# Loading the first chunk's values from ScalarE's queue, and filling a gap of TensorE with four constant products

## The chip, the core and the metric

The kernel runs on one core of a Trainium2 chip. The metric is the device time of one execution in microseconds (us). Five engines work side by side, each through its own instructions in order: TensorE (PE; its weight loads are shown apart as PEld), VectorE (DVE), ScalarE (ACT), GpSimd (POOL) and SyncE (SP), whose instructions here are nearly all transfers (DMAs). Engines wait for one another and for transfers on semaphores.

## What is computed

An attention whose heads are mixed before and after the softmax, and behind it two layers of weights each with an activation of its own:

```python
# batch 2, 12 heads, sequence 448, head size 64
scores = scale * np.matmul(q, k.transpose(0, 1, 3, 2))
scores = np.einsum('bhij,hg->bgij', scores, w_pre)      # premix
attn = softmax(scores)
attn = np.einsum('bhij,hg->bgij', attn, w_post)         # postmix
x = np.matmul(attn, v)                                   # then 896 tokens x 768
h = x @ w1_in;  x = (h * np.clip(h + 3, 0, 6) / 6) @ w1_out
h = x @ w2_in;  out = (P(h) / (Q(h) + 1e-06)) @ w2_out
```

All inputs are float32. A product of two float32 operands is done as three products of their high and low parts.

## The kernel before

The attention is cut into eight chunks: four of up to 120 query rows for each batch. Chunk C is cut into groups of ten rows (twelve groups in chunks 0 to 2, nine in chunk 3); a group holds 10 rows x 12 heads = 120 partitions, so that the mixing of heads is one product with a 120 x 120 matrix. Groups are counted through all chunks as m: chunk 0 has m = 0 to 11, chunk 1 begins with m = 12.

For each chunk, `scores` makes the products of queries and keys for two heads at a time (tiles `sc`); ACT and DVE copy them to a staging tile `stg`, and two DMAs on SP's queue (line 249, `spread`) rearrange them into the tile `full`, in which the twelve heads of a group lie on 120 partitions. Twelve such DMAs of 210 KB make the `full` of a chunk. Only for chunk 0 they go another way: one DMA for each group (line 252), out of a tile `stage`. The six pairs of heads of chunk 1 are called stg_0 to stg_5 below; the first three are made ahead of the loop over groups (`FIRST = 3`, line 503).

A step of the loop takes one group: `gsplit` (POOL, lines 290 and 292) splits group m+3 of `full` into `sh` and `sl`; `premix` (PE, lines 302 to 304, tile `M`) mixes the heads of group m; DVE takes the maximum (line 306), ACT the exponential `e` (line 308) and the scaled weights `wr` (line 321); `postmix` (PE, line 337, tile `A`) mixes group m-2. Work for the next chunk (its `scores`) and for the chunk before (`av_unit`, line 359: the product with the values, tile `X`) is dealt to steps by small tables. The order on every engine is that of the code (`manual_schedule`) from here on.

The first split of each chunk reads `full`, whose last spreads must have landed: POOL waits there for all of the chunk's spreads.

The values `vraw` are loaded for pairs of heads, 224 KB each, into four buffers (`load_v`, line 130). The first four loads, for chunk 0, are issued on SP's queue in step 3 of chunk 1 (line 596); the fifth and later ones follow as `av_unit` gives a buffer back. The first `av_unit` of chunk 0 runs in step 7 of chunk 1.

The DMAs of all queues are dealt to eight lanes (semaphores `DMAHW0` to `DMAHW7`) in turn, at the time the program is built. A DMA is issued only when the DMA that had its lane before it has landed; the wait stands on the issuing engine, in its order.

Ahead of everything, eleven bf16 products on a constant tile `warm` run on PE (line 150). Between the last `scores` made ahead and the first `premix`, PE waits for the first group's spread and split.

Of the kernel before, what the change touches and what calls it, by code (L numbers as in the profile page):

```python
# [7 lines left out]
F32 = mybir.dt.float32  # L8
# [11 lines left out]
B, H, S, D = 2, 12, 448, 64  # L20
# [9 lines left out]
def plan():  # L30

    chunks, parts = [], []
    for b in range(B):
        for c in range(NCH):
            n = min(CH, S - c * CH)
            G = (n + GR - 1) // GR
            parts.append([(0, G)])
            chunks.append((b, c * CH, n, G))  # L40
    return chunks, parts
# [7 lines left out]
def fused_kernel(  # L49
# [15 lines left out]
    nc = tc.nc  # L65
    NT, DM = out.shape
    DFF = w1_out.shape[0]
    WARM = 11
    KD = DM // 128
    KF = DFF // 128  # L70
    GLAG = 1
# [1 line left out]
    chunks, parts = plan()  # L73
# [30 lines left out]
    ps = tc.alloc_tile_pool(name="ps", bufs=2, space=PSUM)  # L104
# [22 lines left out]
        nc.sync.dma_start(out=t, in_=k[b, :, 2 * m : 2 * m + 2])  # L127
        kraw[(b, m)] = t

    def load_v(C, hp):  # L130
        if C < len(chunks) - 1:
            t = att.tile([JP, 2, JC * D], F32, tag="vraw", bufs=4, name=f"vraw{C}_{hp}")
            nc.sync.dma_start(out=t, in_=v[chunks[C][0], hp])
            vraw[(C, hp)] = t

    def load_vs():
# [9 lines left out]
    warm = front.tile([128, 512], BF16, name="warm")  # L146
    nc.vector.memset(warm, 0.0)
    pw = ps.tile([128, 512], F32, tag="A", name="warm_ps")
    for i in range(WARM):
        nc.tensor.matmul(pw, lhsT=warm[:, :128], rhs=warm, start=(i == 0), stop=(i == WARM - 1))  # L150
    for m in range(3):
# [6 lines left out]
    for i, w in enumerate((w_pre, w_post)):  # L158
        nc.sync.dma_start(
            out=wrep[:, i, :], in_=w[None, :, :].to_broadcast([GR, H, H])  # L160
# [52 lines left out]
    def room(n):  # L213
        while posts and sum(banks_of) + n > BUFS["sc"]:
            banks_of.pop(0)
            for p in posts.pop(0):
                p()

    def post(n, *parts):
        banks_of.append(n)  # L220
        posts.append(parts)

    def flush():
        room(BUFS["sc"] + 1)
        while xposts or preps:
            for p in (xposts or preps).pop(0):
                p()
# [9 lines left out]
    def q_prep(C, p0=0, p1=NP):  # L237
        ns = chunks[C][3] * GR
        hi, lo, src = (x[:, p0:p1, :ns] for x in (qr, ql, qraw[C]))
        preps.append([  # L240
            lambda: nc.scalar.activation(out=hi, in_=src, func=AF.Copy),
            lambda: nc.vector.tensor_tensor(out=lo, in0=src, in1=hi.bitcast(F32), op=ALU.subtract),
        ])
# [10 lines left out]
    def scores(C, hp, tags=("sc", "sc"), st=None, first=nc.scalar.copy,  # L254
               second=nc.vector.tensor_copy):
        n = chunks[C][3] * GR
        kh, kl = kst[:, 0, hp, :], kst[:, 1, hp, :]
        if hp == 0:
            full[C] = att.tile([GP, MG, S], F32, tag="full", bufs=2, name=f"full{C}")
        room(2)  # L260
        sc = [ps.tile([128, 512], F32, tag=t, bufs=BUFS[t], name=f"sc{C}_{2 * hp + i}") for i, t in enumerate(tags)]
        far = st is None
        if far:
            st = front.tile([CH, 2, S], F32, tag="raw", bufs=5, name=f"stg{C}_{hp}")
        for j, (w, x) in enumerate(((qr, kh), (ql, kh), (qr, kl))):
            for i in range(2):
                o = slice(i * D, i * D + D)
                nc.tensor.matmul(sc[i][:n, :S], lhsT=w[o, hp, :n], rhs=x[o], start=(j == 0), stop=(j == 2))  # L268

        def take(i, copy):  # L270
            copy(out=st[:n, i], in_=sc[i][:n, :S])
            if far:
                spread(C, 2 * hp + i, st[:, i])

        post(2, lambda: take(0, first), lambda: take(1, second))

    ssp = {}

# [225 lines left out]
    q_prep(1, 0, FIRST)  # L504
    flush()
    for hp in range(FIRST):
        scores(1, hp)
        flush()
    q_prep(1, FIRST, NP)
    flush()  # L510
    gsplit(0, nc.vector)()
# [14 lines left out]
    def gemm1(f, p, hp):  # L526
        hps[(f, p)] = hp
        return gemm_in(p, hp, spl[("in1", f, 0)])
# [40 lines left out]
    for C, (b, r0, n, G) in enumerate(chunks):  # L569
        nxt = C + 1 if C + 1 < len(chunks) else None  # L570
        sched = {}

        def add(units, steps):
            for i, u in enumerate(units):
                sched.setdefault(steps[i * len(steps) // len(units)], []).append(u)

        sst = SST[G] if C else ONES
        if nxt is not None:
            kw = {} if C else {"first": nc.vector.tensor_copy}
            add([lambda h=h: scores(nxt, h, **kw) for h in range(0 if C else FIRST, NP)], sst)  # L580
        if C + 2 < len(chunks):
            add([lambda: q_prep(C + 2, 0, NP // 2), lambda: q_prep(C + 2, NP // 2, NP)], QST[G] if C else [6, 8])
        if C == NCH - 2:
            add([lambda m=m: load_k(1, m) for m in range(3)], [6, 7, 9])
            add([lambda h=h: k_prep(1, h) for h in range(4)], [9, 10, 10, 11])
        if C == NCH - 1:
            add([lambda h=h: k_prep(1, h) for h in range(4, NP)], [0, 1])
        if C > 0:
            add([lambda h=h: av_unit(C - 1, h) for h in range(1, H, 2)], [("av", a) for a in (AVST[G] if nxt is not None else AVLAST)])

        for s in range(G):
            if s == (5 if C == 1 else 0) and C and C + 2 < len(chunks):
                load_q(C + 2)
            if C == 1 and s == 3:
                for i in range(4):
                    load_v(0, i)
            if C == 2 and s == 3:
                load_ab()
            if C == 3 and s == 0:
                build_ab()  # L600
            while aposts:
                aposts.pop(0)()
            if full_step:
                norm(m - 1)
                weigh(m - 1)
            for p in posts[:1] + xposts:
                p[0]()
            gsplit(m + 3)()
            if C:
                for p in posts[:1]:  # L610
                    p[1]()
            premix(m)
            if m == 0:
                low()
            if not C:
                for p in posts[:1]:
                    p[1]()
            if m >= 1 and not full_step:
                norm(m - 1)
                weigh(m - 1)  # L620
            for p in posts[1:]:
                p[0]()
            for p in posts[1:]:
                p[1]()
            full_step = bool(s in sst if nxt is not None else s >= 7) or ("av", s) in sched
            for p in xposts + lows:
                p[1]()
            for p in preps:
                p[0]()
            lows[:] = preps  # L630
            preps.clear()
            xposts.clear()
            posts.clear()
            banks_of.clear()
            if C > PRE or (C == PRE and s == G - 1):
                next(wpieces)
            if m >= LAG:
                postmix(m - LAG)
            for u in sched.get(("av", s), []):
                u()  # L640
            for u in sched.get(s, []):
                u()
            if C == PRE and s == LATE - 1:
                flush()
                front.release()
                pools["late"] = tc.alloc_tile_pool(name="late", bufs=1, side="right", reuse_waits="tile")
                load_units(1)
                wpieces = (p for u in units[:4] for p in split_pieces(u))
            if C == PRE and s >= LATE:
                x_move(s - LATE, 0, XEAR)  # L650
            if C > PRE and s < KD - 3:
                x_move(s + 3, 0, XEAR)
            if C > PRE and s == 3:
                x_move(slice(0, KD), XEAR, XRAW)
            if C > PRE and s == 1:
                load_vs()
            if C > PRE and s == 4:
                load_units(2)
            if nxt is None and s >= 7:
                if s == 7:  # L660
                    h100 = gemm1(0, 0, ps.tile([128, 512], F32, tag="sc", bufs=BUFS["sc"], name="h1_0_0"))
                for _ in range(3):
                    next(h100)
            m += 1

    C = len(chunks) - 1
# [77 lines left out]
    for c in range(KD):  # L744
        hp = [bank(f"y1_{c}_{p}") for p in range(2)]
# [76 lines left out]
    for f in range(KF):  # L822
        advance(ui)
        w = spl.pop(("in2", f, 0))
# [8 lines left out]
        hp = hps[0]  # L833
# [5 lines left out]
        if f == 0:  # L839
            hp = hps[1]  # L840
            run(gemms[1])
        else:
            hp = bank2(tags[1], f"h2_{f}_1")
# [54 lines left out]
    for t in range(NB0):  # L898
        o = gp.tile([TB, DM], F32, tag="o", bufs=3, name=f"o0_{t}")
# [15 lines left out]
    for t in range(NB1):  # L915
        row = P0 + t * TB
        o = gp.tile([TB, DM], F32, tag="o", bufs=3, name=f"o1_{t}")
# [61 lines left out]
```

## Time and profile before

| | |
|---|---|
| median of three runs | 713.1 us (712.63 to 716.39) |
| the profiled execution | 713.87 us, its span 712.1 us |
| PE busy in the span | 696.0 us (98%) |
| DVE, ACT, POOL busy | 558.1, 412.3, 256.0 us |
| DMA queue of SP | 121.66 MB, 54.2% of 16 engines' span |
| mean granted clock of TensorE | 0.994 of full speed |

The busy time of PE says little by itself, since products are pipelined and their ends are modelled. What matters here is where PE stands still, what it waits for there, and the two places in the attention where its granted clock is at half.

### The profile page before, as it was taken

The page shows a single profiled execution, that of the slowest core. Times are in us where ns is not written, and L with a number is a line of the kernel's source. Part 1 is how long each engine was busy: PE and PEld are TensorE (multiplying, and loading weights), DVE is VectorE, ACT ScalarE, POOL GpSimd, SP SyncE. Part 2 cuts the span into 40 slices and gives each one's busy share as a digit, 9 for nine tenths or more (in the row PEclk, how much of TensorE's full clock was granted, in tenths as well). Part 3 has the DMA queues.
Part 4 walks back from the last instruction along what each step waited for, and adds up shares of the span by engine and source line. Part 5 has one row for each costly group of instructions (what it writes and reads, how often), then busy time and mean ns, then how long its engine had stood idle before and what let it go on. Part 6 is the DMA issues. An engine that isn't in the chain of part 4 may idle for free.

```text
span 712.1 us, 12398 instructions
## 1 busy us (share of the span) xinstructions
PE 696.0 (98%) x4457; PEld 620.7 (87%) x4457; DVE 558.1 (78%) x933; ACT 412.3 (58%) x851; POOL 256.0 (36%) x255
## 2 busy tenths in 40 slices
PE   8998999999999999999999999999999999999997
PEld 4778888888889888989888888879999999989997
DVE  6754675665657589899997777888988899899991
ACT  6776787777888443435332211246676767579851
POOL 2884864977776334332444443410000000000000
PEclk9999999999999999999999999999999999999999
DMA  6636486555394454555354554364657666855522
GB/s 201 228 98 184 129 209 181 165 145 177 108 250 139 129 160 133 155 156 156 119 185 142 183 183 140 115 208 169 210 192 240 214 230 212 310 187 200 185 83 88
DMA packets 76032, 122.81 MB, mean 172 GB/s; under 512 B 6804, under 2 KB 56260, under 8 KB 75972
## 3 DMA queue, kind: packets, MB, share of 16 engines
q1 hardware_dynamic: 75684, 121.66, 54.2%
q8 instruction: 35, 0.57, 0.4%
q10 hardware_dynamic: 288, 0.37, 0.1%
q14 instruction: 25, 0.20, 0.1%
HBM read 83.39 MB, written 19.27 MB: 144 GB/s over the span
## 4 chain that ended last, share of the span: by engine, by line
PE 47%; DVE 31%; DMA 10%; issue 5%; ACT 5%; POOL 0%; SPq 0%; ACTq 0%; DVEq 0%; POOLq 0%
PE A L337 9%; DVE wf L431 7%; DVE wf L427 7%; PE X L359 5%; PE acc L385 4%; PE sc L268 4%; PE acc L384 4%; PE acc L383 4%; DMA pre<-wf 4%; DVE gl L550 4%; DVE wf L425 4%; DMA wraw<-in_moe_w_in_dram 4%; PE M L302 3%; PE h L384 3%; PE h L385 3%
## 5 line engine op out<-in xcount | busy, mean ns | idle before, releaser
L385 PE MATMUL h<-xh,wl 128*128 128x512 f32 (+1 forms) x384 | 140.9, 367 | 0.8 <-DVE wl L451 0.7
L384 PE MATMUL h<-xl,wh 128*128 128x512 f32 (+1 forms) x384 | 140.8, 367 | 0.5 <-DVE xl L759 0.5
L383 PE MATMUL h<-xh,wh 128*128 128x512 f32 (+1 forms) x384 | 141.1, 367 | 0.0
L423 ACT ACTIVATE wf<-wraw 128x768 f32<-128x768 f32 (+1 forms) x56 | 48.6, 877 | 96.6 <-DMA pre<-wf 56.5
L292 POOL TENSOR_TENSOR sl<-full,sh 120x448 fp32r<-120x448 f32 x87 | 99.9, 1149 | 7.3
L306 DVE TENSOR_REDUCE st<-M 120x1 f32<-120x448 f32 x90 | 56.0, 622 | 53.9 <-PE M L304 53.6
L337 PEld LDWEIGHTS A<-wr,e 120*112 120x112 f32 x720 | 87.4, 178 | 7.4 <-ACT wr L321 3.1
L337 PE MATMUL A<-wr,e 120*112 120x120 f32 x720 | 89.5, 268 | 1.7 <-ACT wr L321 1.7
L447 POOL TENSOR_SCALAR wh<-wf 128x768 fp32r<-128x768 f32 (+1 forms) x34 | 32.6, 960 | 140.7 <-DVE wf L431 135.1
L308 ACT ACTIVATE e<-M,st 120x448 f32<-120x448 f32 x90 | 57.1, 634 | 41.8 <-DVE st L306 34.8
L385 PEld LDWEIGHTS h<-xh,wl 128*128 128x128 f32 x384 | 72.2, 188 | 10.2 <-DVE wl L451 1.7
L384 PEld LDWEIGHTS h<-xl,wh 128*128 128x128 f32 x384 | 72.2, 188 | 8.7 <-DVE xl L759 0.9
L383 PEld LDWEIGHTS h<-xh,wh 128*128 128x128 f32 x384 | 72.2, 188 | 8.0
L385 PE MATMUL y<-gh,wl 128*128 128x384 f32 x192 | 70.9, 369 | 1.1 <-POOL wl L448 1.1
L290 POOL TENSOR_SCALAR sh<-full 120x448 fp32r<-120x448 f32 x87 | 53.3, 612 | 49.9 <-PE M L303 19.8
L383 PE MATMUL y<-gh,wh 128*128 128x384 f32 x192 | 70.5, 367 | 0.0
L384 PE MATMUL y<-gl,wh 128*128 128x384 f32 x192 | 69.9, 364 | 0.0
L448 POOL TENSOR_TENSOR wl<-wf,wh 128x768 fp32r<-128x768 f32 (+1 forms) x34 | 67.7, 1990 | 2.8
L427 DVE SCALAR_TENSOR_TENSOR wf<-wraw,icst,wf 128x768 int32<-128x768 int32 (+1 forms) x56 | 61.8, 1103 | 1.0
L425 DVE TENSOR_SCALAR wf<-wf 128x768 int32<-128x768 int32 x66 | 42.4, 642 | 23.0 <-ACT wf L423 22.4
L431 DVE SCALAR_TENSOR_TENSOR wf<-wraw,icst,wf 128x768 int32<-128x768 int32 (+1 forms) x56 | 57.7, 1031 | 0.6
L549 ACT ACTIVATE gh<-g 128x384 fp32r<-128x384 f32 (+1 forms) x32 | 18.6, 581 | 60.3 <-DVE g L547 59.9
(109 smaller groups left out, 1524.2 us busy)
## 6 DMA issues: line engine op xcount, KB each, us to landing
wraw<-in_moe_w_out_dram SPq DMA_DIRECT2D x28, 768.0 KB
wraw<-in_moe_w_in_dram SPq DMA_DIRECT2D x22, 768.0 KB
full<-stg SPq DMA_DIRECT2D x60, 210.0 KB
vraw<-in_v_dram SPq DMA_DIRECT2D x42, 224.0 KB
wpre<-in_moe_w_in_dram SPq DMA_DIRECT2D x10, 768.0 KB
w2h<-wh SPq DMA_DIRECT2D x16, 384.0 KB
w2l<-wl SPq DMA_DIRECT2D x16, 384.0 KB
wsh<-w2h SPq DMA_DIRECT2D x16, 384.0 KB
```

What stands on the lines that cost most here:

```text
L290: eng.tensor_scalar(out=sh[:r], in0=s[:r], scalar1=1.0, scalar2=0.0, op0=ALU.mult, op1=ALU.add)
L292: return lambda: eng.tensor_tensor(out=sl[:r], in0=s[:r], in1=sh[:r].bitcast(F32), op=ALU.subtract)
L306: nc.vector.tensor_reduce(out=st[:r, 0:1], in_=mt[:r, :S], op=ALU.max, axis=AX.X, negate=True)
L308: nc.scalar.activation(out=e[:r], in_=mt[:r, :S], func=AF.Exp, bias=st[:r, 0:1], accum_out=st[:r, 1:2])
L337: nc.tensor.matmul(av[:, jc], lhsT=e[:r, jc * JP : (jc + 1) * JP], rhs=wr[:r, :, :rr], start=True, stop=True)
L383: nc.tensor.matmul(o, lhsT=wh, rhs=mh, start=first, stop=False)
L384: nc.tensor.matmul(o, lhsT=wh, rhs=ml, start=False, stop=False)
L385: nc.tensor.matmul(o, lhsT=wl, rhs=mh, start=False, stop=last)
L425: nc.vector.tensor_scalar(out=wi, in0=wi, scalar1=3, scalar2=None, op0=ALU.logical_shift_left)
L427: nc.vector.scalar_tensor_tensor(out=wi, in0=hw, scalar=icst[:, 0:1], in1=wi, op0=ALU.bitwise_and, op1=ALU.bitwise_or)
L431: nc.vector.scalar_tensor_tensor(out=wi, in0=lw, scalar=icst[:, 1:2], in1=wi, op0=ALU.logical_shift_right, op1=ALU.bitwise_or)
L448: nc.gpsimd.tensor_tensor(out=lv, in0=w, in1=hv.bitcast(F32), op=ALU.subtract)
```

## The change

Two edits. The first four loads of values are issued on ScalarE's queue at the end of the last step of chunk 0 instead of on SP's queue in step 3 of chunk 1. And four bf16 products on the constant tile `warm`, with 512 columns each, are put behind the last product of the `scores` made ahead; `issue_after` ties them to that place of PE's order.

```diff
-    WARM = 11
+    WARM, GAP = 11, 4
-    def load_v(C, hp):
+    def load_v(C, hp, eng=nc.sync):
...
-            nc.sync.dma_start(out=t, in_=v[chunks[C][0], hp])
+            eng.dma_start(out=t, in_=v[chunks[C][0], hp])
...
     for hp in range(FIRST):
-        scores(1, hp)
+        mm = scores(1, hp)
         flush()
+    pw = ps.tile([128, 512], F32, tag="A", name="gap_ps")
+    with tc.issue_after(mm.ins):
+        for i in range(GAP):
+            nc.tensor.matmul(pw, lhsT=warm[:, :128], rhs=warm, start=(i == 0), stop=(i == GAP - 1))
...
-            if C == 1 and s == 3:
-                for i in range(4):
-                    load_v(0, i)
...
+            if C == 0 and s == G - 1:
+                for i in range(4):
+                    load_v(0, i, nc.scalar)
```

On SP's queue, the spreads of stg_2 to stg_5 of chunk 1 (rows 24 to 31 of that queue) with the semaphores for which each waits. Before:

```order
L249 DMA full_270<-stg_2_299 10x12x448 [waits DMAHW4_49,Activation_49]
L249 DMA full_270<-stg_2_299 10x12x448 [waits DMAHW5_49,DVE_49]
L249 DMA full_270<-stg_3_356 10x12x448 [waits DMAHW6_49,DVE_49]
L249 DMA full_270<-stg_3_356 10x12x448 [waits DMAHW7_49,DVE_49]
L249 DMA full_270<-stg_4_413 10x12x448 [waits DMAHW0_49,DVE_49]
L249 DMA full_270<-stg_4_413 10x12x448 [waits DMAHW1_49,DVE_49]
L249 DMA full_270<-stg_5_470 10x12x448 [waits DMAHW2_49,DVE_49]
L249 DMA full_270<-stg_5_470 10x12x448 [waits DMAHW3_49,DVE_49]
```

The same eight rows in the changed kernel:

```order
L249 DMA full_270<-stg_2_299 10x12x448 [waits DMAHW0_49,Activation_49]
L249 DMA full_270<-stg_2_299 10x12x448 [waits DMAHW1_49,DVE_49]
L249 DMA full_270<-stg_3_361 10x12x448 [waits DMAHW2_49,DVE_49]
L249 DMA full_270<-stg_3_361 10x12x448 [waits DMAHW3_49,DVE_49]
L249 DMA full_270<-stg_4_418 10x12x448 [waits DMAHW4_49,DVE_49]
L249 DMA full_270<-stg_4_418 10x12x448 [waits DMAHW5_49,DVE_49]
L249 DMA full_270<-stg_5_475 10x12x448 [waits DMAHW6_49,DVE_49]
L249 DMA full_270<-stg_5_475 10x12x448 [waits DMAHW7_49,DVE_49]
```

The order on SP is the same, but every one of these spreads has moved by four lanes: four DMAs have been dealt lanes 4 to 7 between stg_1 (lanes 0 to 3) and stg_2.

On ACT, in the changed kernel, the rows around the four loads; `e_611` and `wr_615` belong to m = 11 and m = 10, the last of chunk 0, and `e_641` to m = 12, the first of chunk 1:

```order
L309 ACTIVATE e_611,st_609<-M_605,st_609 120x448 [waits DVE_49]
L322 ACTIVATE wr_615<-wq,st_586 120x120 [waits DVE_49,Activation_49]
L133 DMA vraw_0_622<-in_v_dram 112x512 [waits DMAHW4_49]
L133 DMA vraw_1_624<-in_v_dram 112x512 [waits DMAHW5_49]
L133 DMA vraw_2_626<-in_v_dram 112x512 [waits DMAHW6_49]
L133 DMA vraw_3_628<-in_v_dram 112x512 [waits DMAHW7_49]
L309 ACTIVATE e_641,st_639<-M_635,st_639 120x448 [waits DVE_49]
```

These are the four DMAs that hold lanes 4 to 7. In the built program the count for which stg_4's first spread waits on lane 4 is 64, and the load vraw_0 waits there for 48 and brings it to 64; so the load has the lane ahead of the spread, and likewise vraw_1 to vraw_3 ahead of the three spreads behind it.

On PE, in the changed kernel, the end of the scores made ahead and the first premix:

```order
L268 MATMUL sc_5_298<-xh,qr 120x448
L513 LDWEIGHTS warm
L513 MATMUL gap_ps<-warm 128x512
L513 LDWEIGHTS warm
L513 MATMUL gap_ps<-warm 128x512
L513 LDWEIGHTS warm
L513 MATMUL gap_ps<-warm 128x512
L513 LDWEIGHTS warm
L513 MATMUL gap_ps<-warm 128x512
L303 MATMUL M_334<-sh_317,wp_h 120x448 [waits DVE_49,Pool_49]
```

Before, the row of `M` stood directly behind that of `sc_5`; the four products wait for nothing.

## Rows read from the trace of the kernel before

**Rows 1.** The page: span and instructions.

```profile
span 712.1 us, 12398 instructions
```

**Rows 2.** PE's timeline (start, us, engine, line, out<-in, count [idle before <-releaser]), 1 to 28 us.

```profile
1.24 4.87 PE L150 MATMUL warm_ps<-warm 128*128 128x512 bf16 x11 [1.24 <-DVE icst L172]
...
15.35 0.44 PE L302 MATMUL M<-sh,wp_h 120*120 120x448 f32 x1 [1.00 <-DVE sh L290]
...
17.39 0.68 PE L268 MATMUL sc<-xh,qr 64*120 64x448 f32 x2
...
21.19 0.44 PE L302 MATMUL M<-sh,wp_h 120*120 120x448 f32 x1
...
22.79 0.46 PE L268 MATMUL sc<-xh,qr 64*120 64x448 f32 x2
...
25.04 0.44 PE L302 MATMUL M<-sh,wp_h 120*120 120x448 f32 x1
```

**Rows 3.** Stretches: busy us of PE, PEld, DVE, ACT, POOL; granted clock, DMA share, GB/s.

```profile
14.00:15.00 1.00, 0.35 (x3) 0.00 (x0) 0.19 (x1) 0.53 (x1) 0.00 (x0) 1.00 0.65 251
...
18.00:19.00 1.00, 1.00 (x7) 0.44 (x4) 0.76 (x3) 0.66 (x3) 0.92 (x2) 0.50 0.66 244
```

**Rows 4.** POOL's timeline, the first split of chunk 1.

```profile
37.59 0.56 POOL L290 TENSOR_SCALAR sh<-full 120x448 fp32r<-120x448 f32 x1 [3.73 <-PE A L337]
```

**Rows 5.** Stretches around the first split of chunk 1, columns as in rows 3.

```profile
36.00:37.00 1.00, 1.00 (x10) 0.91 (x9) 0.24 (x2) 0.85 (x4) 0.00 (x0) 1.00 0.05 18
37.00:44.00 7.00, 5.72 (x40) 4.02 (x38) 3.65 (x13) 4.13 (x12) 6.08 (x8) 1.00 0.01 4
```

**Rows 6.** PE's timeline at the first group of chunk 1.

```profile
38.21 0.46 PE L302 MATMUL M<-sh,wp_h 120*120 120x448 f32 x1 [0.65 <-POOL sh L290]
...
39.43 0.47 PE L304 MATMUL M<-sl,wp_h 120*120 120x448 f32 x1 [0.56 <-POOL sl L292]
```

**Rows 7.** SP's timeline: issues of transfers (start, us, line, count), from several stretches.

```profile
0.79 0.39 SPq L157 DMA_DIRECT2D kraw<-in_k_dram  x1
...
11.95 0.86 SPq L252 DMA_DIRECT2D full<-stage  x1
...
29.18 0.76 SPq L249 DMA_DIRECT2D full<-stg  x1
...
31.74 0.85 SPq L249 DMA_DIRECT2D full<-stg  x1
...
48.47 1.89 SPq L133 DMA_DIRECT2D vraw<-in_v_dram  x4
```

**Rows 8.** ACT's timeline at the end of chunk 0.

```profile
38.06 0.39 ACT L321 ACTIVATE wr<-wq,st 120x120 f32<-120x120 f32 x1
```

**Rows 9.** First readers of a key load and of a group's spread, ACT's and DVE's timelines.

```profile
3.69 0.58 ACT L233 ACTIVATE xh<-kraw 128x448 fp32r<-128x448 f32 x1 [0.70 <-DMA kraw<-in_k_dram]
14.81 0.39 DVE L290 TENSOR_SCALAR sh<-full 120x448 fp32r<-120x448 f32 x1 [0.85 <-DMA full<-stage]
```

**Rows 10.** PE's timeline, 64 to 73 us and 87 to 91 us.

```profile
67.78 2.65 PE L359 MATMUL X<-at,vraw 112*64 112x120 f32 x32 [2.00 <-DMA vraw<-in_v_dram]
...
72.61 0.44 PE L302 MATMUL M<-sh,wp_h 120*120 120x448 f32 x1
...
87.51 1.86 PE L359 MATMUL X<-at,vraw 112*64 112x120 f32 x32
...
90.75 0.44 PE L302 MATMUL M<-sh,wp_h 120*120 120x448 f32 x1
```

**Rows 11.** Stretches ahead of that wait and behind it, columns as in rows 3.

```profile
48.40:66.00 17.60, 17.38 (x166) 15.44 (x164) 9.99 (x30) 13.56 (x38) 9.92 (x12) 1.00 0.82 226
...
69.00:70.00 1.00, 1.00 (x14) 1.00 (x12) 0.00 (x0) 0.00 (x0) 0.92 (x3) 0.50 0.11 20
```

**Rows 12.** The chain of work that ended last, in order of time.

```profile
58.81 8.92 DMA vraw<-in_v_dram
...
67.78 2.65 PE X L359 x32
```

More of the change, by code (lines that the diff above doesn't have):

```diff
@@ L267, in scores @@
                 o = slice(i * D, i * D + D)
-                nc.tensor.matmul(sc[i][:n, :S], lhsT=w[o, hp, :n], rhs=x[o], start=(j == 0), stop=(j == 2))
+                mm = nc.tensor.matmul(sc[i][:n, :S], lhsT=w[o, hp, :n], rhs=x[o], start=(j == 0), stop=(j == 2))
         def take(i, copy):
@@ L275, in scores @@
         post(2, lambda: take(0, first), lambda: take(1, second))
+        return mm
     ssp = {}
```

## The prediction

> **What bounds the kernel now.** The page gives the span, 712.1 us [rows 1]; the profiled execution took 713.87 us, so 1.8 us lie around the span. The median of the three runs shown is 713.1 us, 0.8 below it. The sum below is made against 713.87. I then followed PE through the first 75 us, where both edits act, looked at each of its stops, and asked of each what came last.
>
> The first stop is ahead of the first premix: PE is idle for 1.00 us until 15.35 us, when the first split is ready [rows 2]. Two microseconds after it works again, its granted clock is at half, 1.2 of 2.4 GHz (0.50 at 18 to 19 us) [rows 3]. That slows it: from the products `sc` at 17.39 us to the second `M` behind them at 21.19 us it takes 3.80 us, and for the same work at full clock (22.79 to 25.04 us) 2.25 us [rows 2]. The dip costs PE 1.55 us of its own time.
>
> The second stop is at the first group of chunk 1. PE waits for POOL's split, which starts at 37.59 us [rows 4], 0.65 us and then 0.56 us [rows 6]. The reader is to see what POOL waited for there. The row names PE, but that split reads `full` of chunk 1, so it needs all twelve spreads; the DMA engines fall nearly still just before (share 0.05 at 36 to 37 us, 0.01 from 37 to 44 us) [rows 5], and the last spread was issued at 31.74 us [rows 7]. I read the wait as one for the landing of that spread. It decides the next step: what happens to PE ahead of 37.6 us is worth nothing beyond 0.65 us as long as that landing stays, and everything behind it moves if the landing moves.
>
> The third stop is 2.00 us ahead of `X` at 67.78 us [rows 10]; the chain of waits runs through it: a load of values issued at 58.81 us lands 8.92 us later [rows 12], because the DMA engines were 0.82 busy for 17 us ahead of it [rows 11]. Behind this stop the clock is at half again [rows 11], and from that `X` to the second `M` behind it PE takes 4.83 us, where the same work at full clock takes 3.24 us (87.51 to 90.75 us) [rows 10]: 1.59 us more.
>
> **The change part by part.**
>
> *The four products.* The eleven ahead of everything took 4.87 us, 0.44 us each [rows 2]; at that price four take 1.77 us, 0.77 us more than the gap, at half of it (full clock is granted at 14 to 15 us [rows 3]) 0.89 us, which fits. I take the second. Then PE has no gap, and I expect no dip at 17.4 us. PE does not win 1.55 us of the kernel by it: the cover is the landing at 37.6 us, and it would stop there longer. Direct worth 0 (from +0.8 with the long products to -0.65). It counts only through how early ACT comes to its loads: ACT's work in these steps waits for PE, but also for DVE and POOL; of 1.55 us I let half, 0.8 us, arrive there.
>
> *The loads, where they stand now.* The four loads on ACT stand behind `wr` of m = 10, which starts at 38.06 us [rows 8]; with 0.8 us won, ACT issues the first at about 37.3 us. By the lanes, the first spread of stg_4 cannot be issued on SP until this load has landed, and the other three spreads of stg_4 and stg_5 wait for the three other loads. Before, these four spreads were issued between 29.18 and 31.74 us [rows 7]. So the change adds a wait of some 11 us to SP's queue, and what is queued behind it is the rest of `full` of chunk 1, for which POOL's first split waits, for which PE waits.
>
> Priced: a load on quiet engines, issue to first reader, took 2.90 us (0.79 to 3.69 us), a spread 2.86 us (11.95 to 14.81 us) [rows 7, 9]. The first load lands at 37.3 + 2.9 = 40.2 us. Four spreads are issued 0.85 us apart (three times that is 31.74 - 29.18 = 2.56 us [rows 7]); the loads are 0.47 us apart on SP (four in 1.89 us [rows 7]), so only the first load holds them, and the last spread goes out at 42.8 us. To the split it takes 2.86 us on quiet engines and took 5.85 us in the full queue before (31.74 to 37.59 us) [rows 4, 7]; the engines are quiet but for the loads, so I take 3.3 us. The split then starts at 46.1 instead of 37.59 us: **+8.5 us**. From below: ACT gains all 1.55 us (36.5), then 2.9, 2.56 and 2.86 make 44.8, +7.2 us. From above: ACT gains nothing and issues behind the end of its `wr` (38.45), then 2.9, 2.56 and 5.85 make 49.8, +12.2 us.
>
> *PE restarts from a long stop.* A stop of 1 or 2 us was followed by half clock, which cost 1.55 and 1.59 us. PE now stands still for some 9 us. Behind 38.2 us PE still waits for POOL (0.56 us of it is in [rows 6]), which hides part: I take +1.0 us, from 0 (all hidden) to 3.2 (two such dips, none hidden).
>
> *The loads, where they stood.* Without them, 0.92 MB (4 x 224 KB) leave the stretch 48.4 to 66 us, which moves 226 GB/s [rows 11]: 4.1 us of transfer. The load that landed at 67.73 us would then come some 4 us earlier relative to PE, and PE needs it 2.0 us earlier. The stop and its dip go: 2.00 + 1.59 = **-3.6 us**. If the loads ahead of the stop are held by something else, nothing is won (0).
>
> A rule of the Trainium skill bears on this part (DMA: Bandwidth & Descriptors, Issuing engines are not separate DMA queues): transfers from all queues run on the same DMA engines, and spreading them over queues saves no more than the issuing time. By it alone the second part would be worth at most the 1.89 us that SP no longer spends, and the sum 1.7 us higher, 721.5 us. The rows here speak for the larger figure, not because the queue is another but because the bytes move into a quiet stretch.
>
> **Sum:** 713.87 + 8.5 + 1.0 - 3.6 = **719.8 us**, 0.8% above. Behind 38 us the chain of waits runs through PE with the same relative distances, so I see nothing that would take this back. Since the profiled execution lies 0.8 us above the median, I put the time at 719.6 us. Bounds of the terms together: +7.2 + 0 - 3.6 = +3.6 (717.5) and +12.2 + 3.2 - 0 = +15.4; not all ends come together, the upper least.
>
> **The rivals.**
>
> 1. *The lanes do not hold the spreads up* (faster). It is decided by one point: whether the loads land before SP comes to stg_4 at 29.18 us. They would have to be issued by ACT by 26.3 us. Against it stands ACT's order: `wr` of m = 10 ran at 38.06 us, and only an ACT that reaches its DMAs out of order could do it. Then the stop at 67.8 us goes and nothing comes: 713.9 - 3.6 = 710.3 us; with 0.65 us at 38.2 us at most 709.6. Chance 0.06.
>
> 2. *The new stop is covered* (about the same). That is, POOL's split did wait for PE, as its row says, or the split's own wait is not what PE's later work hangs on. Then only a part of the 8.5 us comes through; 3.6 us cancels against the second part: 712 to 716 us. Against it: what PE has to give back for that split is the buffer of m = 9, three groups earlier; and PE's row at 38.21 us names POOL [rows 6]. Chance 0.06.
>
> 3. *The stop is longer or costs more clock.* The spreads land at the slow end, or PE runs at half clock for two dips, or the stop at 67.8 us stays because something else than the four loads held it: 713.9 + 8.5 + 3.2 - 1.9, or + 12.2 + 1.0 - 3.6, or + 8.5 + 1.0: 723.4 to 723.7 us. Speaks for it: no row shows a load and spreads together on engines that have just fallen still, nor PE's restart from so long a stop. Chance 0.18.
>
> The forecast itself: 0.70.
>
> **How the numbers follow.** The forecast's own range, 717.5 to 722.3 us, holds most of 0.70. To leave out no more than 2 in 10, I reach to rival 3's ends: 716.9 to 723.7 us; what stays out is rivals 1 and 2 and the far upper corner. Within 0.5% of the median, about what a measurement of this kernel can tell from no change, is 709.5 to 716.7 us. Rival 1 lies at that edge: half of it (0.03) counts as faster, half as the same, together with rival 2 and a thin low end of the forecast: 0.11. Slower: 0.86.
>
> **What would show it.** In the changed profile: the fourth-last spread of chunk 1 is issued on SP not at 29 but at about 40 us, behind a wait of some 11 us; the DMA share falls to about zero between 34 and 38 us; POOL's first split of chunk 1 starts near 46 us and PE's first `M` of chunk 1 right behind it, with an idle of some 9 us in front; full clock from 15 to 35 us, half clock behind that idle; no wait for `vraw` in front of the third `X` of chunk 0. If the split still starts near 38 us, the reading of the lanes is wrong, and the time is near 710. If the split comes at 46 but the time is still near 714, something behind took it back that I have not seen.

## The result and the profile after

The changed kernel takes 720.95 us (median of six runs, 719.46 to 721.96), the kernel before on the same chip 714.03 us (six runs, 712.27 to 716.39): a ratio of 1.009 (95% interval 1.0069 to 1.0111). It is slower, by 6.9 us. The profiled execution took 721.96 us, the slowest of the six; its span is 720.2 us, 8.1 us above that of [rows 1].

Line numbers of `gsplit`, `premix`, `postmix` and `av_unit` are one higher than before (291, 303, 338, 360). The first view to read is PE's waits in the first 110 us: engine, line and operand waited for, then us in total, times, and the longest.

```profile
PE M L303 <- POOL sh L291: 10.8, 1, 10.8
PE A L338 <- ACT wr L322: 1.3, 3, 0.5
```

One wait of 10.8 us has come, and the 2.0 us at `X` are no longer in the list. The chain of waits says what the 10.8 us are (start, duration, what ended last there):

```profile
37.36 0.64 DVE st L307
...
38.02 0.27 ACT e L309
...
38.36 0.34 ACTq L133
...
39.22 3.96 DMA vraw<-in_v_dram
...
43.25 0.76 SPq L249
```

ACT comes to the loads at 38.36 us, only when the premix of the last group of chunk 0 has been through DVE and its exponential has begun on ACT. The third load, issued at 39.22 us, lands 3.96 us later, and with it ends a wait of SP, which then issues the third of its four spreads (line 249, at 43.25 us). SP's row for these four, POOL's first split of chunk 1, and on PE the first `M` of chunk 1 and the first `sc` behind it (start, duration, instruction, idle time in front and what ended it):

```profile
41.08 3.78 SPq L249 DMA_DIRECT2D full<-stg  x4
```

```profile
48.27 0.57 POOL L291 TENSOR_SCALAR sh<-full 120x448 fp32r<-120x448 f32 x1 [13.57 <-DMA full<-stg]
```

```profile
48.89 0.73 PE L303 MATMUL M<-sh,wp_h 120*120 120x448 f32 x1 [10.75 <-POOL sh L291]
...
54.27 0.47 PE L268 MATMUL sc<-xh,qr 64*120 64x448 f32 x2
```

In the kernel before that `sc` came 4.45 us behind its `M` (38.21 us [rows 6]):

```profile
42.66 0.47 PE L268 MATMUL sc<-xh,qr 64*120 64x448 f32 x2
```

They answer to [rows 4, 6, 7]: spreads that had been issued from 29.18 us now go out from 41.08 us, and the split starts 10.68 us later (48.27 against 37.59 us). The row of POOL now names the DMA itself. The windows show the pause and the clock (width, busy us of PE, PEld, DVE, ACT and POOL, granted clock, DMA share, GB/s):

```profile
36.00:37.00 1.00, 1.00 (x10) 0.91 (x9) 0.60 (x2) 1.00 (x4) 0.00 (x0) 1.00 0.00 0
38.00:39.00 1.00, 0.14 (x2) 0.00 (x0) 0.80 (x3) 0.98 (x3) 0.00 (x0) 1.00 0.00 0
40.00:41.00 1.00, 0.00 (x0) 0.00 (x0) 0.00 (x0) 0.00 (x0) 0.00 (x0) 1.00 0.99 354
44.00:52.00 8.00, 2.99 (x10) 2.30 (x11) 0.85 (x3) 0.47 (x1) 3.56 (x5) 0.50 0.27 86
52.00:54.00 2.00, 2.00 (x13) 1.82 (x12) 0.44 (x1) 1.05 (x4) 1.92 (x3) 0.66 0.00 0
58.00:75.60 17.60, 17.60 (x171) 15.51 (x171) 9.44 (x29) 13.80 (x38) 11.06 (x14) 1.00 0.69 201
```

The transfer engines do nothing until the loads start, and PE, which is still, gets half clock from 44 us until some 4 us into its new work. The last row is the stretch of work that [rows 11] showed from 48.4 to 66 us: as there, it ends 1.8 us ahead of the third `X` of chunk 0, which now comes about 9.6 us later. Its DMA share is 0.69 instead of 0.82. PE's rows of the first `X` and around the third, which has no wait:

```profile
67.68 1.86 PE L360 MATMUL X<-at,vraw 112*64 112x120 f32 x32
...
77.36 1.86 PE L360 MATMUL X<-at,vraw 112*64 112x120 f32 x32
...
80.59 0.44 PE L303 MATMUL M<-sh,wp_h 120*120 120x448 f32 x1
```

A row of 32 products `X` is two pairs of heads, so the third needs the fifth load of values, which is not one of the four that were moved; SP issues it once the first `X` has given a buffer back. The first `X` and SP's row of the fifth and later loads, before:

```profile
56.05 1.86 PE L359 MATMUL X<-at,vraw 112*64 112x120 f32 x32
```

```profile
58.81 11.96 SPq L133 DMA_DIRECT2D vraw<-in_v_dram  x6
```

After:

```profile
69.09 5.63 SPq L133 DMA_DIRECT2D vraw<-in_v_dram  x4
```

So the fifth load starts 1.41 us behind the first `X` instead of 2.76 us.

### The profile page after: what moved, and what is told of

Its sections match the earlier page's. It is cut to its first block, busy times and chain, and to the rows that moved or that the text cites. A ratio compares the mean times of both kernels' runs of the same rounds, so it can differ in the third digit from the quotient of the medians.

```text
span 720.2 us, 12404 instructions
## 1 busy us (share of the span) xinstructions
PE 696.3 (97%) x4460; PEld 620.8 (86%) x4461; DVE 557.2 (77%) x933; ACT 413.1 (57%) x851; POOL 256.8 (36%) x255
## 4 chain that ended last, share of the span: by engine, by line
PE 45%; DVE 31%; DMA 13%; issue 5%; ACT 5%; SPq 0%; POOL 0%; ACTq 0%; DVEq 0%; POOLq 0%
PE A L338 9%; DVE wf L432 7%; DVE wf L428 7%; PE X L360 5%; PE acc L386 4%; PE acc L385 4%; PE acc L384 4%; DMA pre<-wf 4%; DVE gl L555 4%; DVE wf L426 4%; PE sc L268 3%; PE M L303 3%; DMA wraw<-in_moe_w_in_dram 3%; PE h L385 3%; PE h L386 3%
```

## The experiments

Diffs are against the changed kernel. In the results, "split" is POOL's first split of chunk 1, "PE's wait" the wait in front of the first `M` of chunk 1.

**First set: the two edits apart, and two kernels with clean lanes.** *Products alone*, the loads back on SP in step 3 of chunk 1:

```diff
+            if C == 1 and s == 3:
+                for i in range(4):
+                    load_v(0, i)
...
-            if C == 0 and s == G - 1:
-                for i in range(4):
-                    load_v(0, i, nc.scalar)
```

> The four products alone; the loads stand on SP's queue in step 3 of chunk 1 as before. Lane theory (the loss comes from the spreads of stg_4 and stg_5 waiting for the loads that hold their lanes): no loss, POOL's first split of chunk 1 at about 37.6 us, no half clock between 17 and 21 us, the stop at X and its dip still there, time within 0.7 us of before (ratio 0.999 to 1.000). Rival, the products cost PE or delay the first premix: 1 us or more above before.

*Loads alone*, without the products:

```diff
-    pw = ps.tile([128, 512], F32, tag="A", name="gap_ps")
-    with tc.issue_after(mm.ins):
-        for i in range(GAP):
-            nc.tensor.matmul(pw, lhsT=warm[:, :128], rhs=warm, start=(i == 0), stop=(i == GAP - 1))
```

> The move of the loads alone, without the four products. Lane theory: the whole loss, 7 to 9 us above before (ratio 1.009 to 1.012), the split at 47 to 49 us. Rival, the products bring the loss: near before, or 3.6 us below it since the stop at X goes.

*The same place, SP's queue*:

```diff
-                    load_v(0, i, nc.scalar)
+                    load_v(0, i)
```

> The changed kernel with the four loads at the same place of the program, but on SP's queue; the lanes of stg_4 and stg_5 are then those of the kernel before. Lane theory: the split back at about 37.6 us, no stop at X at 68 us, 3 to 4 us below before (ratio 0.994 to 0.996). Rival, the place is bad by itself because 0.92 MB then compete with the last spreads: the split 2 to 4 us late, time about that of before.

*ScalarE's queue, one step later*:

```diff
-            if C == 0 and s == G - 1:
+            if C == 1 and s == 0:
```

> The changed kernel with the four loads still on ACT's queue, one step later (step 0 of chunk 1, three rows down in ACT's order); they then get lanes behind those of stg_4 and stg_5. Lane theory: the split at about 37.6 us, the loads issued at about 41 us and landed by 46 us, no stop at X, 3 to 4 us below before (ratio 0.994 to 0.996). Rival, ACT's queue is what costs (its own transfers or its issuing time of 1.9 us): a loss of several us remains.

Measured, beside 714.3 us for the kernel before:

| | us | ratio (95%) | split, us | PE's wait, us |
|---|---|---|---|---|
| products alone | 712.0 | 0.9964 (0.9937 to 0.9992) | 39.84 | 2.4 |
| loads alone | 721.06 | 1.0094 (1.0065 to 1.0122) | 47.23 | 10.8 |
| same place, SP's queue | 712.03 | 0.9966 (0.9949 to 0.9983) | 40.38 | 3.2 |
| ScalarE's queue, a step later | 709.26 | 0.9924 (0.9903 to 0.9946) | 37.78 | 1.8 |

The loads alone lose all that the change loses. The queue does not do it, since the same four loads a step later on the same queue are the fastest kernel of the study. What the two slow kernels share and the others don't is that the loads have lanes 4 to 7 ahead of the spreads; that it is not their bytes is shown by the second set. At the same place on SP's queue the rival was half right: SP issues the loads from 33.92 us, they share the engines with the last spreads (DMA share 0.98 at 36 to 37 us), and the split is 2.8 us later than in the kernel before, though part of that belongs to a slow first spread (last section). The gain of 2.3 us is short of the 3 to 4 expected. Products alone were 2.3 us faster, which I had not expected; the third set comes back to it.

**Second set: lanes without bytes, and an earlier issue.** *Tiny transfers on the lanes* (adds 7 KB of values that nobody reads; the real loads go back to SP, as above):

```diff
-                    load_v(0, i, nc.scalar)
+                    nc.scalar.dma_start(out=tiny[:, i], in_=v[0, 0, :, 0, :4])
```

> Four tiny transfers (112 x 4 values each, read by nobody) stand on ScalarE's queue where the change has its loads and take lanes 4 to 7 there; the real loads stay on SP in step 3 of chunk 1, and the four products are kept. Theory (lanes): the lanes alone make the stop. ACT issues the first tiny transfer at about 38.4 us, it lands some 2 us later, four spreads 0.85 us apart and some 3.5 us of landing follow: the first split of chunk 1 starts at about 46.5 to 47.5 us, PE idles 9 to 10 us there, and the stop of about 2 us at X of chunk 0 stays, because the real loads are back in the busy stretch. Against the run with the products alone (712.0 us): + 9.3 + 0.9 = 722 us, ratio about 1.011 (1.007 to 1.014), as slow as the change itself or slower. Rival (the bytes of the loads hold the spreads up on the transfer engines, not the lanes): 7 KB hold nothing up, split at 37.5 to 39.5 us, 712 us, ratio 0.997.

*The loads two steps earlier*:

```diff
-            if C == 0 and s == G - 1:
+            if C == 0 and s == 9:
```

> As the change, but the four loads stand on ScalarE's queue at the end of step 9 of chunk 0 instead of step 11; they still take lanes 4 to 7 ahead of stg_4 and stg_5. Theory (lanes): the stop follows ACT's issue of the first load one for one. ACT comes to it some 4 us earlier (about 34 us), so the split starts at about 44 us instead of 48.3, PE idles about 6.5 us instead of 10.8, and the time is 721 - 4 = 717 us, ratio 1.004 (1.001 to 1.007). Rival (any load of values in front of the spreads costs the same, by its bytes): no smaller than the change's loss, 721 us, ratio 1.009. Rival (the loads are far enough ahead): split at 38 us, 709.5 us, ratio 0.993.

With the tiny transfers the kernel takes 723.14 us, before 712.53 us: ratio 1.0135 (1.0089 to 1.0181). Its chain of waits (line numbers one higher, since a line was added for the tile):

```profile
37.52 1.53 DMA tiny<-in_v_dram
...
39.11 0.76 SPq L250
...
40.82 0.76 SPq L250
...
41.67 4.09 DMA full<-stg
```

A transfer of 1.8 KB lands 1.53 us after its issue, and in that moment SP issues a spread; the split starts at 45.94 us. PE's waits there, and at the `X` of before, where the real loads are again late:

```profile
PE M L304 <- POOL sh L292: 9.3, 1, 9.3
PE X L361 <- DMA vraw<-in_v_dram: 2.2, 1, 2.2
```

So the lanes alone make the stop (9.3 of the 10.8 us: the small transfers land sooner), and without the move of the bytes nothing is given back: this is the slowest kernel.

Two steps earlier: 717.91 us, ratio 1.0063 (1.0034 to 1.0091). ACT's first load, POOL's split and PE's first `M`:

```profile
33.43 0.34 ACTq L133 DMA_DIRECT2D vraw<-in_v_dram  x1
```

```profile
43.35 0.56 POOL L291 TENSOR_SCALAR sh<-full 120x448 fp32r<-120x448 f32 x1 [9.51 <-DMA full<-stg]
```

```profile
43.97 0.73 PE L303 MATMUL M<-sh,wp_h 120*120 120x448 f32 x1 [6.58 <-POOL sh L291]
```

The load is issued 4.93 us earlier than in the changed kernel (33.43 against 38.36 us), and the split starts 4.92 us earlier (43.35 against 48.27 us): one for one in these two executions. The medians give back less: 3.0 us, and only 1.5 us when each is taken beside the kernel before on its own chip (5.4 us above it instead of 6.9). The profiled execution is the fastest of ten that spread over 7 us (714.83 to 721.74); what the slower ones lost has no profile.

**Third set: what are the products worth?** *A step later, no products* (the two diffs above for these, together):

> The kernel with clean lanes (four loads on ScalarE's queue at the end of step 0 of chunk 1; 709.26 us with the products) without the four products. Theory (the products save something of their own, 2.3 us as when they stood alone): the two gains add up, this one is at 709.3 + 2.3 = 711.6 us, ratio about 0.9960. Rival (the products are worth nothing, as the prediction had it; the 2.3 us were chance or belong to where the loads stood): 709.3 to 710.3 us, ratio 0.993 to 0.9945, the 3.6 us of the stop at X and its dip alone giving 710.7, ratio 0.995.

*Products alone, once more*:

> The products alone once more, for a profile of another execution. Theory (the products save something of their own): about 712.0 us again, ratio 0.9965 (0.994 to 0.999); no stretch at half clock between 16 and 25 us, and the spreads of stg_3 to stg_5 issued 1 to 2 us earlier than the 28 to 31.7 us of before, with the first split of chunk 1 at 35.5 to 37 us. Rival (worth nothing, as predicted): 714 us, ratio 1.000, split at 37.6 us, PE waiting there 0.65 us or longer.

They took 711.5 us, ratio 0.999 (0.9968 to 1.0012), and 712.84 us, ratio 1.0002 (0.9978 to 1.0027). The first time is the one that the theory of a saving had named, but its ratio lies above both forecasts, because the kernel before took only 712.53 us on that chip. In the products alone the gain of 2.3 us did not come again; the split, at 40.07 us, was later than either forecast. Then three kernels side by side, beside 713.5 us before: *a step later, once more*; *a step later, on SP's queue*; *a step later, no products, once more*.

> The kernel with clean lanes (four loads on ScalarE's queue at the end of step 0 of chunk 1, with the four products) once more, beside the two others of this set on one chip. The removed stop at X and its dip alone: 713.3 - 3.6 = 709.7 us, ratio 0.995 (0.992 to 0.998). Against the same kernel without the products (e7: 711.5 us on another chip): theory (the products are worth nothing, PE only stops longer at the first M of chunk 1): within 0.7 us of that kernel; rival (they save 2 us of their own): 2 us below it.

> As e9, but the four loads at that place stand on SP's queue: the same bytes at nearly the same time, lanes 4 to 7 clean (behind all spreads of chunk 1's full), only the queue differs. Theory (it is when the bytes move and which lanes they take, not whose queue issues them): the same as e9 within 0.7 us, ratio 0.995, no stop at X of chunk 0. Rival (ScalarE's queue itself saves or costs something: 1.9 us of SP's issuing): 1.9 us above e9, ratio 0.9975, with the spreads of chunk 2 later on SP.

> e9 without the four products, on the same chip. Theory (the products are worth nothing): within 0.7 us of e9, first M of chunk 1 at 38 to 38.5 us in both. Rival (they save 2 us): 2 us above e9, as the 711.5 us on another chip had it.

They took 709.94 us, ratio 0.9948 (0.9926 to 0.997); 711.48 us, 0.9964 (0.9942 to 0.9986); and 711.28 us, 0.9964 (0.9939 to 0.999). All three beat the kernel before. Both others missed the 0.7 us of their forecasts: they lie 1.5 and 1.3 us above the first. The intervals overlap, but seven of the first's twelve runs are under 710 us, and only two and one of the others', so that the first is likely the faster. SP, which runs ahead, had come to its loads at 32.40 us, so that kernel differs from the first in when the bytes move as well as in the queue; it does not test the queue alone.

What the products do to the clock can be compared where two executions are alike ahead of the split: the kernels a step later, with products (span 708.2 us) and without (708.1 us), each in its first profile. Windows and PE's first `M` of chunk 1, with products:

```profile
17.00:20.00 3.00, 2.49 (x15) 1.53 (x15) 2.40 (x9) 2.13 (x6) 2.48 (x3) 1.00 0.66 244
40.00:42.00 2.00, 2.00 (x12) 1.68 (x11) 0.85 (x3) 1.01 (x3) 1.83 (x4) 0.64 0.03 8
42.00:44.00 2.00, 2.00 (x11) 1.78 (x12) 0.85 (x3) 0.91 (x2) 1.92 (x3) 0.51 0.88 251
```

```profile
38.40 0.46 PE L303 MATMUL M<-sh,wp_h 120*120 120x448 f32 x1 [1.77 <-POOL sh L291]
```

And without:

```profile
17.00:20.00 3.00, 3.00 (x11) 2.00 (x11) 2.40 (x8) 2.13 (x6) 2.46 (x3) 0.55 0.66 243
40.00:42.00 2.00, 1.93 (x14) 1.27 (x13) 1.09 (x4) 1.01 (x3) 1.92 (x3) 1.00 0.13 30
42.00:44.00 2.00, 2.00 (x19) 1.51 (x17) 0.38 (x3) 0.60 (x2) 1.92 (x3) 1.00 0.74 214
```

```profile
38.05 0.46 PE L303 MATMUL M<-sh,wp_h 120*120 120x448 f32 x1 [0.65 <-POOL sh L291]
```

The products take the half clock at 17 to 20 us away; in all nine profiles with products the granted clock is 1.00 there. PE arrives earlier, waits 1.77 instead of 0.65 us, and behind that longer stop gets half clock at 40 to 44 us, which it does not get without them. In this pair the dip is not removed but moved behind the wait. It isn't always so. In the second profiles of the same two kernels the clock is at full at 17 to 20 us in both: without products PE stood still for 0.95 us ahead of the first premix, and no dip followed. Both then wait long at the first `M` of chunk 1 (3.05 us with products, 2.79 without) and both get half clock behind it. And in the products alone there is no half clock in either place, in either profile.

What this is worth in time can be read at the third `X` of chunk 0, behind both dips. In the first pair, with products and without:

```profile
66.91 1.86 PE L360 MATMUL X<-at,vraw 112*64 112x120 f32 x32
```

```profile
65.96 1.86 PE L360 MATMUL X<-at,vraw 112*64 112x120 f32 x32
```

And in the second:

```profile
69.38 1.86 PE L360 MATMUL X<-at,vraw 112*64 112x120 f32 x32
```

```profile
69.34 1.86 PE L360 MATMUL X<-at,vraw 112*64 112x120 f32 x32
```

The products have won nothing there: the kernel without them is 0.95 us ahead in the first pair and level in the second, and at the last `X` of the attention it is 0.9 and 0.7 us ahead. The spans of the second pair (711.8 and 713.7 us) differ the other way by what comes behind: from the last `X` to the end the thirteen profiles took 477.6 to 480.8 us, in work that neither edit touches.

## Why the prediction was right

**The lanes (chance 0.70): right.** The changed profile has the signs named ahead: the four spreads at 41.08 us (about 40 forecast) behind a wait of more than 9 us, a DMA share of nearly zero ahead of the loads, the split late, half clock behind the idle, and no wait at the third `X`. One differs: full clock was to come from 15 us and came at 16, since this execution had half clock at 13 to 15 us, ahead of the products. That it is the lanes is shown from three sides: the same bytes and queue off these lanes cost nothing, four transfers of 1.8 KB on them make a stop of 9.3 us, and an issue 4.93 us earlier brings the split 4.92 us earlier.

**The stop: right in kind, too small.** +10.7 us against +8.5, inside the bounds of 7.2 and 12.2. Of the 2.2 us, 1.06 are ACT's issue (38.36 against 37.3 us). The 0.8 us that I let PE's saving pass to ACT is shown by no run: with products ACT comes to this place at 38.36 us here and at 37.52 with the tiny transfers, but earliest, at 37.22 us, in the loads alone, which have no products. The place differs from execution to execution by more than that. Here the first grouped transfer of chunk 0 had gone out 0.7 us late (12.67 instead of 11.95 us), and `wr` of m = 10 started at 38.65 instead of 38.06 us, 0.3 us behind the first load's issue. The load's landing was as forecast (2.72 us from issue to the first freed spread; 2.9). 0.46 us more came from the third load: I had only the first one hold the spreads, but the third, with other loads and two spreads in flight, took 3.96 us (4.05 in the loads alone). And the last spread took 4.17 us to the split (44.10 to 48.27 us) where I took 3.3; the chosen value was too near its lower end. It isn't the loads' bytes: with the tiny transfers it took 4.27 us (41.67 to 45.94 us).

**PE's restart: right.** From the first `M` of chunk 1 to the `sc` behind it PE takes 5.38 us (48.89 to 54.27) where before it took 4.45 (38.21 to 42.66): +0.93, forecast +1.0.

**The stop at X: right in size, in part for another reason.** From the first `M` of chunk 1 to the second `M` behind the third `X`: 34.40 us before (38.21 to 72.61), 31.70 after (48.89 to 80.59), 2.70 less. With the 0.93 us of the restart in it, the stop and its dip gave 3.63 us; forecast 3.6. The three terms make 10.68 + 0.93 - 3.63 = +8.0 us, the span +8.1; in between, at the last `X` of the attention, the difference is 7.4 us (233.81 and 241.24), so that the last half microsecond agrees by chance. By the rule of the Trainium skill (DMA: Bandwidth & Descriptors, Issuing engines are not separate DMA queues) taken alone this part was bounded by 1.89 us of issuing; the trace exceeds it, and both kernels with the loads on SP's own queue have lost the stop too (no wait at the third `X`). That agrees with the rule's first half, that a second queue is no second set of engines. But the forecast put the whole gain down to bytes that leave the stretch, and issuing has a share: SP, with four loads fewer ahead of it, comes to the fifth load 1.35 us earlier behind the first `X` (1.41 instead of 2.76 us). Of the 2.00 us of waiting this leaves at least 0.65 us to a faster landing (at most 8.27 us, 69.09 to 77.36, instead of 8.92) in a stretch with a DMA share of 0.69 instead of 0.82. No run parts the two further; the dip of 1.6 us went with the wait.

**The products: no effect that could be made sure of.** The forecast was zero, hidden behind the landing at 37.6 us. In the changed kernel that holds: 720.95 us with them, 721.06 without (other chips, ratios 1.009 and 1.0094). The first pair of profiles shows the cover, and adds what I had not seen, the dip moving along. Elsewhere the medians leave it open: products alone gave -2.3 us once and +0.3 us once. With clean lanes the kernels with them were lower both times, by 2.2 us (other chips, and the intervals of the two ratios do not overlap) and by 1.3 us (same chip, overlapping). Taken alone that would be a gain of 1 to 2 us, against the forecast; but in the two pairs of profiles the kernel without products is 0.95 us ahead or level when both dips are past, and the layers behind the attention alone take up to 3 us more in one execution than in another. So no profile shows a saving, and whether the other executions hold one stays open.

**The rivals.** "The lanes do not hold the spreads up" fell with the split at 48 us; its price was near the mark, since kernels with the loads moved and clean lanes come to 709.3 to 712.0 us where it had 709.6 to 710.3. "The new stop is covered" fell with PE's wait of 10.8 us. The longer stop was half true: a slower landing, but only one dip, and the stop at `X` did go. The predicted 719.6 us lies 1.4 us below the median; the term that was too small is the stop.

## What to carry to other kernels

Where transfers are dealt to a few completion semaphores, a transfer moved to another queue can hold up transfers of a third party: look, for each moved transfer, at who has its lane next, and when the issuing engine comes to it. Here the same edit one step later in the code turned a loss of 0.9% into a gain of 0.5 to 0.8%. Work put into a gap of PE is worth what the next wait leaves of it; if that wait is set by a queue, the time can be lost there instead, and in one pair of profiles here the clock was too.

## What the hardware showed besides

The issue of SP's first spread behind the grouped transfers differs from execution to execution, and the start of chunk 1 with it. The row in the kernel before, and in the second run of the products alone:

```profile
21.89 0.81 SPq L249 DMA_DIRECT2D full<-stg  x1
```

```profile
21.82 1.81 SPq L249 DMA_DIRECT2D full<-stg  x1
```

In the four profiles with clean lanes where it takes 0.81 us, the split starts at 37.4 to 38.6 us; in the five where it takes 1.4 to 2.0 us, at 39.8 to 40.4 us (the latest of each set is a kernel with the loads on SP, whose bytes then run beside the spreads). The kernels a step later, profiled twice each, still show it at the third `X` (rows above): 66.91 and 69.38 us with products, 65.96 and 69.34 us without, the later with the slow issue each time. So a slow issue goes with a split some 2 us later and with work behind it that is 2.5 to 3.4 us later, and two single profiles can be compared only where they are alike there. That the issue is the cause isn't tested, and what lengthens it the traces don't tell.

How long PE stands still does not alone tell what clock it gets behind the stop. At the first `M` of chunk 1, waits of 1.77, 2.57, 2.79, 3.05 and 3.17 us (kernels with the loads moved and clean lanes) were followed by half clock, waits of 0.65 (twice) and 0.89 us by full clock. But in the first run of the products alone PE waited 2.42 us, and the granted clock was 1.00 all through, in this stretch and in each to 48 us:

```profile
40.47 0.47 PE L303 MATMUL M<-sh,wp_h 120*120 120x448 f32 x1 [2.42 <-POOL sh L291]
```

```profile
40.00:42.00 2.00, 0.99 (x4) 0.57 (x5) 0.00 (x0) 0.00 (x0) 1.92 (x3) 1.00 0.02 4
```

At the first premix it is the same: half clock followed stops of 0.75, 1.00 and 1.24 us, and not one of 0.95 us. At the third `X`, half clock followed the stop of 2.00 us [rows 10, 11], and not one of 1.56 us in the second run of the products alone.
